# Attention and two MLP layers on one core: a slack before TensorE operations in the planned issue order

## The chip, the cores and the metric

The kernel runs on one core of one Trainium2 chip. The metric is device time in microseconds (us), the median of several runs. A core has five engines that each work through their own queue in order: PE (TensorE, matmuls, with PEld for its weight loads), DVE (VectorE), ACT (ScalarE), POOL (GpSimd) and SP (SyncE, which here issues DMAs). They meet only where one waits for another's result.

## The reference

Attention over 4 batches, 8 heads, 576 positions and 64 dimensions a head. Of each row of scores only those within `tau` of the row's maximum are kept:

```python
scores = scale * np.matmul(q, k.transpose(0, 1, 3, 2))
thresh = np.max(scores, axis=-1, keepdims=True) - tau
scores = np.where(scores >= thresh, scores, -1000000000.0)
attn = np.exp(scores - np.max(scores, axis=-1, keepdims=True))
attn = attn / (np.sum(attn, axis=-1, keepdims=True) + 1e-09)
out = np.matmul(attn, v)
```

The result, 2304 tokens of 512 values, goes through `a = x @ w1; b = x @ w2; x = (a * b @ w3) @ w_out` and then through `h = x @ w_in; x = elu(h) @ w_out2`, with 1024 and 2048 inner columns.

## The kernel before, in words

The attention phase works in 144 tiles of 128 score rows by 576 columns, nine to a pair of heads (16 pairs, `p`), each pair in two parts: n=0 with four tiles, n=1 with five. Four pairs are one batch. The order of the tiles is `SEQ` (lines 329 and 330): the first parts of pairs 0 to 3, then their second parts, then pair by pair.

A tile `i` goes through this chain. S (`emit_S`, matmuls on line 352 for pairs 0 to 3 and on line 364 for the others) writes scores to one of three PSUM buffers `s`. MAX (line 373, VectorE) takes the negated maximum. Two small GpSimd operations make the exponent's bias (line 381, for some tiles) and the threshold (line 377). EXP (lines 386 and 388, ScalarE) and MASK (line 394, VectorE) follow. Then the masked tile is transposed in one of two ways. Most tiles of n=0 go through X (`emit_X`, line 442, five TensorE transposes into the tile's own PSUM buffer) and C (`emit_C`, line 446, a ScalarE copy). Tiles of n=1 of most pairs (`by_dma`) are cast to two halves (line 401 ScalarE, lines 405 and 406 GpSimd) and transposed by DMA (lines 432 and 434, issued by SyncE). In the X way the `s` buffer is free after C, in the DMA way after MASK.

When all tiles of a part are masked, `emit_rr` (lines 454 and 455, VectorE) makes reciprocals of the sums, `turn_r` (line 460, TensorE) turns them, `keep_r` (line 465, ScalarE) copies them out, and SyncE stores them to memory (lines 472 and 474) and loads them back spread over partitions (lines 482 to 488). `emit_PV` (lines 502 and 510, TensorE, in five parts) multiplies with v; `emit_xf` (lines 519 and 521, VectorE) scales by the reciprocals; `emit_xh` (line 527) and `emit_xl` (line 531) split the result for the first MLP layer. The v operand is loaded by `load_v` (line 300), its column sum made by line 305 on ScalarE and brought over partitions by `v_mean` (line 308, TensorE). From pair 4 on, q and k are cast and split (line 284 ScalarE, lines 271, 288 and 292 GpSimd).

The first MLP products ("ab", line 552) of batches 0 to 2 are mixed into the same phase. A product takes 12 matmuls, planned as four operations of three; a batch has 32 of them, 16 for n=0 and 16 for n=1. They need the split results of all four pairs of a batch for that n, and converted weights (lines 205 to 235), and use one of two PSUM buffers `m`, which PV uses as well. They are emptied by line 560 (ScalarE) or line 567 (VectorE). The fourth batch's ab products follow the phase, then the rest (lines 817 to 1095): weights are combined (line 860), the second product (line 1000), and the last two layers (lines 1033 and 1062).

The order of all this is made by `Plan` (lines 57 to 141), in Python, before the kernel is built. Every operation has an engine, an estimated duration `us`, for DMAs a landing time `land`, a priority `key` (lower goes first) and the operations that it depends on. Rings of buffers add dependencies (`take`, `turns`); the two `m` buffers are slots given out when planned (`hold`). `run` then plays the engines forward. Among the operations of an engine that can start at the earliest time (within 0.05 us) it takes the one with the lowest key and issues its instructions (`o.fn()`). When an operation ends, each one that uses it may start no earlier than its end plus `LAT` = 0.15 us across engines or 0.05 us on the same engine (line 137). So the planned times are turned into nothing but an order: on the chip an engine waits for the semaphores of the next instruction in its queue, and what stands behind waits too.

The keys: S has the tile's number `i`, X `i - 2`, C `i - 3`, MASK `i - 2`, PV the number of the part's last tile plus 5, and the ab products of batch 0 have keys that run from 22 to 46 (n=0) and 46 to 78 (n=1), of batch 1 from 78 to 114, of batch 2 from 114 to 150 (lines 776 to 786).

Of the kernel before, what the change touches and what calls it, by code (L numbers as in the profile page):

```python
# [44 lines left out]
FA, FB, FC = (22.0, 24.0), (46.0, 32.0), (6.0, 36.0)  # L45

LAT = 0.15


class Op:  # L50
# [6 lines left out]
class Plan:  # L57
# [30 lines left out]
    def run(self):  # L88
        self.turns()
        for o in self.ops:  # L90
            o.deps = list({id(d): d for d in o.deps if d is not o}.values())
            o.n = len(o.deps)
            for d in o.deps:
                d.outs.append(o)
        place = {id(o): k for k, o in enumerate(self.ops)}
        ready = {}
        free = {}
        for o in self.ops:
            ready.setdefault(o.eng, [])
            free[o.eng] = 0.0  # L100
            if o.n == 0:
                ready[o.eng].append(o)
        done_at = {}
        left = len(self.ops)
        while left:
            best = None
            for e, r in ready.items():
                cand = []
                for o in r:
                    t = max(free[e], o.at)  # L110
                    if o.gets:
                        n, used = self.slots[o.gets]
                        if len(used) >= n:
                            f = done_at.get(id(used[-n]))
                            if f is None:
                                continue
                            t = max(t, f)
                    cand.append((t, o))
                if not cand:
                    continue  # L120
                t0 = min(t for t, _ in cand)
                t, o = min(((t, o) for t, o in cand if t <= t0 + 0.05), key=lambda x: (x[1].key, place[id(x[1])]))
                if best is None or t < best[0]:
                    best = t, o
            t, o = best
            ready[o.eng].remove(o)
            free[o.eng] = t + o.us
            end = t + o.us + o.land
            if o.gets:
                self.slots[o.gets][1].append(o)  # L130
            if o.frees:
                done_at[id(o.frees[1])] = end + LAT
            o.fn()
            o.start = t
            for x in o.outs:
                x.n -= 1
                x.at = max(x.at, end + (LAT if x.eng != o.eng else 0.05) + x.lag)
                if x.n == 0:
                    ready[x.eng].append(x)
            left -= 1  # L140
        self.end = max(free.values())
# [1001 lines left out]
```

## Time and profile before

| | |
|---|---|
| median of 3 runs | 1067.16 us (1064.76 to 1068.95) |
| the profiled execution | 1067.07 us |
| its span in the trace | 1065.0 us |
| instructions | 17060 |
| PE busy | 1014.1 us (95%) |
| PEld busy | 887.0 us (83%) |
| DVE, ACT, POOL busy | 583.6, 514.0, 441.7 us |

The span is the time from the first to the last instruction of the profiled execution. Busy time of PE counts matmuls from start to a modelled end, so that overlapping ones count once. "Idle before" an instruction is time of its engine that ended when the named releaser, an operation on another engine or a DMA, was done. A row of the timeline gives the start in us from the beginning of the span, the duration of a run of equal instructions, the engine, the line, what it writes and reads, the count, and in brackets the idle time just before it with its releaser. `PEclk` is the share of TensorE's full clock that was granted.

### The profile page before, as it was taken

What the parts mean: (1) busy time and instruction counts of PE and PEld (TensorE: products, weight loads), DVE (VectorE), ACT (ScalarE), POOL (GpSimd) and SP (SyncE); (2) the same over time, 40 slices, a digit from 0 to 9 for tenths busy, and PEclk for the clock granted to TensorE, in tenths of its full rate; (3) what the DMA queues carried; (4) which work ended last, traced back from release to release, by engine and by line L of the source; (5) the groups of instructions that cost most, each with busy time, mean ns of one, the idle gap of its engine ahead of it and who ended that gap; (6) DMA issues with size and microseconds to landing.
All of it is one profiled execution on the core that took longest, in us unless ns stands there. A gap on an engine that the chain in (4) does not pass through costs nothing.

```text
span 1065.0 us, 17060 instructions
## 1 busy us (share of the span) xinstructions
PE 1014.1 (95%) x6318; PEld 887.0 (83%) x6318; DVE 583.6 (55%) x1072; ACT 514.0 (48%) x864; POOL 441.7 (41%) x586
## 2 busy tenths in 40 slices
PE   7878999979999999989999999999999999999998
PEld 4445788867888888889879999989999899899997
DVE  4788888764676666646555565843332333323322
ACT  3776777764666665534334555533232232322322
POOL 1648867765657665413321231332222222222221
PEclk8999999998999999999999999999999999999999
DMA  8227688876559444466617673300000000000000
GB/s 264 90 92 197 133 159 137 138 151 158 112 129 160 122 116 87 102 211 211 218 45 242 190 239 110 119 1 30 1 1 30 1 30 1 2 30 1 30 1 30
DMA packets 119726, 109.70 MB, mean 103 GB/s; under 512 B 88176, under 2 KB 106844, under 8 KB 115036
## 3 DMA queue, kind: packets, MB, share of 16 engines
q1 hardware_dynamic: 115532, 78.97, 31.3%
q10 hardware_dynamic: 4112, 29.66, 8.1%
q8 instruction: 49, 0.80, 0.3%
q14 instruction: 33, 0.27, 0.1%
HBM read 73.73 MB, written 14.23 MB: 83 GB/s over the span
## 4 chain that ended last, share of the span: by engine, by line
PE 58%; DMA 1%; issue 1%; POOL 1%; ACT 1%; DVE 1%; SPq 0%; POOLq 0%; ACTq 0%; DVEq 0%
PE h L1033 19%; PE o L1062 19%; PE x L1000 9%; PE ab L552 6%; PE m L860 4%; DMA rb<-rd 1%; POOL hl L405 0%; PE s L364 0%; DMA th<-g_dr 0%; PE s L442 0%; PE pv L502 0%; PE pv L510 0%; DVE sl L200 0%; POOL hl L406 0%; ACT hl L401 0%
## 5 line engine op out<-in xcount | busy, mean ns | idle before, releaser
L552 PE MATMUL ab<-x,W 128*128 128x256 f32 (+1 forms) x1536 | 232.1, 301 | 3.5 <-DVE xf L521 3.5
L552 PEld LDWEIGHTS ab<-x,W 128*128 128x128 f32 x1536 | 211.0, 190 | 10.2 <-issue 3.8
L1062 PE MATMUL o<-WO,sl 128*128 128x512 f32 x864 | 215.7, 394 | 0.6 <-POOL sl L1054 0.6
L1033 PE MATMUL h<-sl,W 128*128 128x384 f32 x1152 | 215.7, 337 | 0.0
L1033 PEld LDWEIGHTS h<-sl,W 128*128 128x128 f32 x1152 | 202.8, 188 | 8.3
L1054 POOL TENSOR_TENSOR sl<-th,sl 128x384 fp32r<-128x384 f32 x87 | 88.4, 1017 | 266.5 <-ACT sl L1049 266.5
L1062 PEld LDWEIGHTS o<-WO,sl 128*128 128x128 f32 x864 | 161.1, 188 | 30.7 <-POOL sl L1054 1.1
L1042 DVE TENSOR_SCALAR th<-h 128x384 f32<-128x384 f32 x96 | 53.3, 555 | 182.8 <-PE h L1033 182.8
L394 DVE SCALAR_TENSOR_TENSOR e<-s,st,e 128x576 f32<-128x576 f32 x144 | 115.3, 814 | 59.2 <-ACT e L388 31.3
L1043 ACT ACTIVATE th<-th 128x384 f32<-128x384 f32 x96 | 50.4, 525 | 194.5 <-DVE th L1042 194.5
L373 DVE TENSOR_REDUCE st<-s 128x1 f32<-128x576 f32 x144 | 106.0, 748 | 23.5 <-PE s L364 7.3
L1000 PE MATMUL x<-sl,M 128*128 128x384 f32 x576 | 101.1, 337 | 0.5 <-ACT sl L199 0.3
L1000 PEld LDWEIGHTS x<-sl,M 128*128 128x128 f32 x576 | 99.6, 188 | 1.9 <-DVE sl L200 0.8
L405 POOL TENSOR_TENSOR hl<-e,hl 128x512 f16<-128x512 f32 x70 | 83.1, 1188 | 24.4 <-ACT hl L401 24.1
L364 PE MATMUL s<-qk 128*128 128x288 f32 x480 | 83.8, 307 | 8.4 <-DVE e L394 4.5
L388 ACT ACTIVATE e<-s,st 128x576 f32<-128x576 f32 x108 | 77.0, 736 | 27.2 <-DVE st L373 17.0
L1049 ACT ACTIVATE sl<-th 128x384 fp32r<-128x384 f32 x96 | 50.4, 525 | 76.7 <-PE o L1062 46.5
L1047 DVE SCALAR_TENSOR_TENSOR th<-th,h 128x384 f32<-128x384 f32 x96 | 53.1, 554 | 58.2 <-ACT th L1043 58.1
L364 PEld LDWEIGHTS s<-qk 128*128 128x128 f32 x480 | 70.1, 192 | 13.3 <-issue 3.8
L442 PE MATMUL s<-ident,e 128*128 128x128 f32 (+1 forms) x370 | 56.1, 284 | 19.5 <-DVE e L394 19.2
L446 ACT ACTIVATE pt<-s 128x640 f32<-128x640 f32 x74 | 51.5, 700 | 45.0 <-PE s L442 36.1
L442 PEld LDWEIGHTS s<-ident,e 128*128 128x128 f32 (+1 forms) x370 | 38.5, 136 | 37.4 <-DVE e L394 32.4
(89 smaller groups left out, 1200.4 us busy)
## 6 DMA issues: line engine op xcount, KB each, us to landing
rqk<-in_qk SPq DMA_DIRECT2D x24, 576.0 KB
raw_wo<-in_wo ACTq DMA_DIRECT2D x12, 1024.0 KB
th<-g_dr SPq DMA_DIRECT2D x48, 192.0 KB
raw_w<-in_w SPq DMA_DIRECT2D x8, 1024.0 KB
raw_w<-in_w3t ACTq DMA_DIRECT2D x8, 1024.0 KB
raw_win<-in_win ACTq DMA_DIRECT2D x8, 1024.0 KB
vr<-in_v SPq DMA_DIRECT2D x16, 320.0 KB
g_dr<-g SPq DMA_DIRECT2D x16, 320.0 KB
```

Of the source, the lines that this page charges most:

```text
L364: T.matmul(s[:, n, :HS], q, k[:, c:c + HS], start=(x == 0), stop=(x == len(ops) - 1))
L373: V.tensor_reduce(st[i][:, 0:1], sc[i][:, :, :HS], axis=AX.XY, op=ALU.max, negate=True)
L388: A.activation(et[i], sc[i][:, :, :HS], AF.Exp, bias=st[i][:, 2:3] if by_dma(i) else st[i][:, 0:1])
L394: V.scalar_tensor_tensor(et[i], sc[i][:, :, :HS], st[i][:, 1:2], et[i], op0=ALU.is_ge, op1=ALU.mult, accum_out=sm[p][:, pos:pos + 1],)
L405: G.tensor_tensor(t[:, S + 64:], e[:, :512], t[:, :512], op=ALU.subtract)
L442: T.transpose(o[:k, c * P:(c + 1) * P], e[:, c * P:c * P + k], ident)
L552: T.matmul(o[:, :w], wf[:, m, wx, kt, :], x[:, xx, :], start=(kt == 0 and k == 0), stop=(kt == NK - 1 and k == 2),)
L1000: T.matmul(o[:, :TB], M[:, f, mx, e * P:(e + 1) * P], gh[j, f][:, gx, :], start=(k == 0), stop=(k == 23),)
L1033: T.matmul(o[:, :TB], WI[f][:, wx, kt, :], xh[j, kt][:, xx, :], start=(k == 0), stop=(k == 3 * NK - 1),)
L1042: V.tensor_scalar(t, o[:, :TB], 0.0, None, op0=ALU.min)
L1054: (V if jobs else G).tensor_tensor(x[:, 1, :], thin[2 + f % 2], f32(x[:, 0, :]), op=ALU.subtract)
L1062: T.matmul(po[j, t], gg[j, f][:, gx, t * P:(t + 1) * P], WO[f // 2][:, f % 2, wx, :], start=(f == 0 and k == 0), stop=(f == NF2 - 1 and k ...
```

## The change

A second constant, `LAG_PE`, is added beside `LAT`. Where an operation on TensorE uses the result of an operation on another engine, its earliest planned start is put 0.8 us later. Slots of `m` (`hold`) and dependencies among other engines keep their times. No instruction is added or removed, and nothing waits for the 0.8 us on the chip: the plan's times change, and with them the order in which the instructions of each engine are issued.

```diff
 LAT = 0.15
+LAG_PE = 0.8
...
             for x in o.outs:
                 x.n -= 1
-                x.at = max(x.at, end + (LAT if x.eng != o.eng else 0.05) + x.lag)
+                wait = LAG_PE if x.eng == "PE" and o.eng != "PE" else 0.0
+                x.at = max(x.at, end + (LAT if x.eng != o.eng else 0.05) + x.lag + wait)
                 if x.n == 0:
                     ready[x.eng].append(x)
```

## Rows read from the trace of the kernel before

**Rows 1.** Stretches of the span: length, busy time per engine, PEclk, DMA share, GB/s.

```profile
0.00:83.00 83.00, 66.47 (x442) 38.83 (x443) 57.97 (x114) 50.40 (x72) 37.67 (x62) 0.96 0.49 156
83.00:213.00 130.00, 121.53 (x933) 98.65 (x933) 105.99 (x219) 94.57 (x156) 101.14 (x165) 0.99 0.76 148
213.00:248.00 35.00, 27.36 (x188) 22.17 (x187) 21.24 (x48) 21.76 (x36) 24.26 (x42) 0.85 0.67 138
248.00:450.00 202.00, 192.40 (x1519) 170.16 (x1519) 135.37 (x302) 124.51 (x218) 120.69 (x204) 1.00 0.58 124
...
475.00:1065.00 590.00, 584.80 (x3087) 536.42 (x3085) 252.23 (x378) 216.38 (x374) 155.46 (x114) 1.00 0.22 72
```

**Rows 2.** The same stretches, the maximum (line 373) alone: DVE busy, one per tile.

```profile
83.00:213.00 130.00, 35.09 (x48) 0.99 0.76 148
213.00:248.00 35.00, 7.82 (x11) 0.85 0.67 138
248.00:450.00 202.00, 45.99 (x63) 1.00 0.58 124
```

**Rows 3.** The third stretch, the ab products (line 552) alone: PE busy, PEld busy.

```profile
213.00:248.00 35.00, 6.18 (x38) 5.62 (x39) 0.85 0.67 138
```

**Rows 4.** Waits of PE, 83 to 213 us: total, times, longest.

```profile
PE s L442 <- DVE e L394: 3.3, 3, 1.9
PE s L364 <- DVE e L394: 2.1, 2, 1.6
PE s L352 <- DVE e L394: 1.4, 1, 1.4
```

**Rows 5.** Waits of PE, 213 to 248 us.

```profile
PE s L364 <- ACT rt L465: 3.4, 1, 3.4
PE s L442 <- DVE e L394: 2.4, 1, 2.4
```

**Rows 6.** Waits of PE, 248 to 450 us.

```profile
PE s L442 <- DVE e L394: 6.2, 9, 1.2
PE s L364 <- DVE e L394: 2.3, 3, 1.1
```

**Rows 7.** Timeline of all engines, 400 to 404 us, the operations around one wait.

```profile
399.36 1.41 DVE L373 TENSOR_REDUCE st<-s 128x1 f32<-128x576 f32 x2
...
400.41 1.43 POOL L288 TENSOR_TENSOR qk<-rqk,qk 64x576 fp32r<-64x576 f32 x1
...
401.94 0.50 POOL L377 TENSOR_SCALAR st<-st,add 128x1 f32<-128x1 f32 x2
402.24 0.82 DVE L394 SCALAR_TENSOR_TENSOR e<-s,st,e 128x576 f32<-128x576 f32 x1 [1.48 <-POOL st L377]
...
403.93 0.70 ACT L446 ACTIVATE pt<-s 128x640 f32<-128x640 f32 x1 [1.96 <-PE s L442]
```

**Rows 8.** Timeline of PE alone, 400 to 428 us, the same wait.

```profile
403.12 1.50 PE L442 MATMUL s<-ident,e 128*128 128x128 f32 x10 [0.91 <-DVE e L394]
404.38 1.12 PE L552 MATMUL ab<-x,W 128*128 128x320 f32 x6
```

**Rows 9.** Timeline of all engines, 15 to 30 us.

```profile
20.35 0.74 ACT L305 ACTIVATE v<-vr 128x640 f16<-128x640 f32 x1 [3.73 <-DMA vr<-in_v]
...
22.54 2.19 PE L352 MATMUL s<-qkp 128*64 128x288 f32 x8 [4.10 <-ACT pt L446]
```

**Rows 10.** Timeline of all engines, 440 to 470 us, the phase's end.

```profile
460.60 0.55 DVE L521 SCALAR_TENSOR_TENSOR xf<-pv,vst,rb 128x320 f32<-128x320 f32 x1 [4.37 <-DMA rb<-rd]
...
461.20 8.99 PE L552 MATMUL ab<-x,W 128*128 128x320 f32 x49 [3.48 <-DVE xf L521]
```

**Rows 11.** One stretch of the last two layers, columns as in rows 1.

```profile
900.00:925.00 25.00, 25.00 (x128) 22.62 (x127) 8.26 (x15) 7.87 (x15) 5.59 (x6) 1.00 0.00 1
```

**Rows 12.** PV (line 502), 0 to 450 us, by shape: count, busy us, mean ns.

```profile
L502 PE MATMUL pv<-pt,vr 128*64 128x256 f32 x256 | 32.9, 393 | 0.6 <-ACT a L560 0.6
...
L502 PEld LDWEIGHTS pv<-pt,vr 128*64 128x64 f32 x288 | 19.1, 139 | 12.8 <-issue 3.2 <-ACT a L560 0.8 <-ACT qk L284 0.4
```

## The prediction

> **What bounds the kernel now.** I read the stages first: busy time and granted clock in six stretches of the span, cut where the kind of work changes [rows 1], then how many score tiles and how many products of the first MLP layer (ab, line 552) fall into each [rows 2, 3], then who makes TensorE wait in each [rows 4 to 6], and last one such wait instruction by instruction [rows 7, 8]. Line numbers are those of the kernel before.
>
> From 475 us on nothing of the changed order is left; TensorE is busy for practically all of that time, and I take it as fixed. The attention phase, up to about 461 us, falls into four parts [rows 1]. Up to 83 us no ab work exists yet; TensorE is idle for 83.0 - 66.5 = 16.5 us. From 83 to 213 us ab products of the first batch fill in; idle 8.5 us. [...] From 248 to 450 us ab work is always at hand; idle 9.6 us at full clock, VectorE only 67% busy (135.4 of 202). The pace is 130 / 48 = 2.7 us a tile in the second part, 35 / 11 = 3.2 in the third and 202 / 63 = 3.2 in the fourth [rows 2].
>
> So the third part shows something the busy shares hide: with less matmul work per tile the tiles do not go faster. There the chain maximum, exponent, mask, transpose sets the pace, not TensorE, and time saved on TensorE before 213 us can be lost again in this gap. Only between 248 and 450 us does a wait on TensorE cost its own length.
>
> What are these waits? Nearly all are a transpose X (line 442) or a score product S (line 364) for VectorE's mask (line 394): 6.2 us in 9 waits and 2.3 us in 3 from 248 to 450, none above 1.2 us [rows 6]; 3.3 + 2.1 + 1.4 = 6.8 us in 6 waits from 83 to 213 [rows 4]. The one at 403 us shows the mechanism: GpSimd is inside a 1.43 us subtraction of line 288, its small threshold operation (line 377) comes behind it, the mask waits for that until 402.24, and X, next in TensorE's order, stands for 0.91 us [rows 7, 8]. Behind it in the same queue lie six ab matmuls that were ready. The planner had put X directly behind the time at which it believed the mask done, and the chip was later than that.
>
> **The change part by part.** It adds nothing to the chip and removes nothing; it alters the order in which instructions enter the queues. In the plan, a TensorE operation becomes ready 0.8 us after the operation on another engine that it uses, on top of the 0.15 us there before. The planner then gives TensorE another ready operation in that time, if it has one. On the chip no instruction waits for this slack: it turns into work in front of X, S, the turn of reciprocals (line 460), the column mean (line 308) and PV. The six ab matmuls behind the wait at 403 take 1.12 us [rows 8], so 0.8 us is about four matmuls, one planner unit of three and a little.
>
> First term, 248 to 450 us: a wait of 0.8 us or less should vanish, a longer one keep its excess. The nine X waits average 0.69 us and the three S waits 0.77; the longest are 1.2 and 1.1 [rows 6]. Excess of up to 0.4 us in perhaps half of them leaves some 1.6 of 8.5 us. Gain 6.9 us. From both sides: all 8.5 if the queue in front is fuller than planned, 0 if the masks come later by as much.
>
> Second term, 83 to 213 us: at most 0.8 us for each of 6 waits, 4.8 us [rows 4]. By the reading of the gap this time comes back as idle time before 248, since the inputs of the next batch come from the tile chain. I take a gain of 1.0 and keep 0 and 4.8 as ends.
>
> Third, 213 to 248 us: the two waits named there are 3.4 us of S for a ScalarE copy and 2.4 us of X for the mask [rows 5]. With no filler at hand the slack moves little: 0, with 2.4 us either way. What covers the moved operations is ab work; in this stretch that cover is gone, and a PV part put in front of X costs its length.
>
> Fourth, up to 83 us: no ab filler either. The large wait (4.10 us at 22.54) is behind ScalarE, which waited 3.73 us for the load of v [rows 9]. Another order on ScalarE could remove that or make a second one; 0, with 4.1 us either way.
>
> Fifth, the end. After the last mask the reciprocals pass TensorE, go out to memory and come back, and VectorE waits 4.37 us for them; TensorE stands idle for 3.48 us before the next ab [rows 10]. That turn now lies up to 0.8 us deeper in the order: loss 0.8, with 0 and 1.6 as ends (the last S may move too). The change of batch inside the long stretch runs through the same chain but has tiles to work on: loss 0.5, between 0 and 1.6.
>
> The other queues move with it. The copies behind X (ScalarE, line 446), the stores of reciprocals and loads behind them (SyncE), xf and its split are planned later, so casts and conversions go ahead of them. A ScalarE copy that falls behind one cast of q and k loses its length at most; where the ring has room this costs nothing, and if that room is gone it is the slower rival below. The DMA transposes follow GpSimd, which gets no slack, and I leave them at zero; SyncE issues in order, so a store of reciprocals that comes later could hold one up, and this is inside the same rival.
>
> Sum: -6.9 - 1.0 + 0 + 0 + 0.8 + 0.5 = -6.6 us. The profiled execution took 1067.07 us (span 1065.0 and 2.1 around it), 0.1 under the median of 1067.16, so no correction is due: **1060.5 us**, 0.6% faster.
>
> [...] By matmul rows, TensorE in 248 to 450 us has 9.6 us to give [rows 1]. Weight loads are busy for 170.2 of these 202 us, 84.2%, while a stretch that never waits shows 22.62 of 25, 90.5% [rows 11]; the difference over 202 us is 12.6 us. I use matmul rows, because the phase has PV products with 64-column weights, which load in 139 ns where the matmul takes 393 [rows 12], so that weight loads idle there without a loss. [...]
>
> **The rivals.** (1) Nothing net, 1067 us. The slack only moves the waits: ab work brought forward is missing afterwards, the gap at 213 us grows by what was saved before it, and the long stretch gets later masks. For it: the gap, in which the tile chain and not TensorE sets the pace. The change could also fail to do what it says: the slack is not added where an ab group waits for its accumulator (the "m" slots), and where one operation alone is ready the order stays. Against it: in 248 to 450 us there is always filler.
>
> (2) Slower, 1076 us: the ring of three score buffers binds. Today an X tile holds its buffer for S (0.6 us by the planner's own cost in line 605) and then from the maximum at 399.36 to the end of the copy at 403.93 + 0.70 = 404.63 [rows 7], 5.9 us in all, 2.0 a tile with three buffers. A slack before X and one before the next S make it 7.5, or 2.5 a tile, against 2.7 a tile from 83 to 213 us and 3.2 later. So there is 0.2 us of room before 213, and none if anything else delays the loop. The price if it binds there: per turn 1.6 / 3 = 0.53 us for the 4 in 9 tiles with an X, 0.27 for the others. 21 x 0.53 + 27 x 0.27 = 18.4 us for 48 tiles, 11.1 if X tiles alone pay. The later gain stays (pace 3.2 against 2.5). Net of -6.9, +0.8 and +0.5 that is 5.5 to 12.8 us slower, 1073 to 1080. It decides from the point at which the loop takes over 8.1 us (three times 2.7).
>
> (3) Larger gain, 1054.8 us: each wait also drains what is behind it, so that the loss is that of the weight loads. For it: weight loads are 6 points short of the dense stretch [rows 1, 11]. Against it: the PV argument.
>
> **How the numbers follow.** The forecast gets 0.47, its own range being 1054 to 1066; rival 1 0.20; rival 2 0.25; rival 3 0.08. A measurement of this kernel tells about 0.5%, 5.3 us, from no change, so faster means below 1061.8: three quarters of the forecast's chance and all of rival 3, 0.43. Same is the rest of the forecast and rival 1, 0.32. Slower is rival 2, 0.25. The range goes from 1054, where the better ends of terms one and two lie (-8.5 - 4.8 + 0.5), to 1076, the middle of rival 2; what lies outside is half of that rival and a little below.
>
> **What the changed profile would show.** If right: the waits of X and S for the mask between 248 and 450 us fall from 8.5 to under 3 us, ab matmuls stand directly in front of X, the stretch from the start of the second batch's ab to the last score tile shrinks by about 7 us, and the time before it stays within 2 us. If rival 1: the waits fall and the gap before the second batch grows by as much. If rival 2: from 83 to 213 us fewer than 48 tiles are done when the first batch's ab ends, and the gap is longer than 40 us. If the large wait near 22 us is gone or another of its size appears before 83 us, the fourth term was wrong, and by that much the time. What would make the prediction wrong outright is a wait for another releaser (ScalarE's copy, the reciprocals) growing where the mask's shrank.

## The result, and the profile after

The changed kernel takes **1073.61 us** (median of 9 runs, 1070.23 to 1078.79) against 1067.37 for the kernel before beside it: a ratio of 1.006 with a 95% interval of 1.0036 to 1.0083. The forecast was 0.6% faster; it became 0.6% slower. The time lies within the stated range, on the side of rival 2. The profiled execution took 1075.75 us, 2.1 above its median, so its differences to the profile before (8.7 us) are somewhat larger than those of the medians (6.2 us). Ratios and their intervals, here and below, leave out two runs that fell into a slow state, one of the kernel before (1079.45 us) and one of experiment 7 (1647.38 us). In the changed kernel all lines of the attention phase have numbers higher by two: MAX is line 375, MASK 396, X 444, C 448, the turn of reciprocals 462, ab 554.

The stretches of [rows 1], in the changed kernel (length, busy time of PE, PEld, DVE, ACT, POOL, granted clock, DMA share, GB/s):

```profile
0.00:83.00 83.00, 66.35 (x408) 39.23 (x408) 56.10 (x106) 47.48 (x68) 29.99 (x61) 0.88 0.48 155
83.00:213.00 130.00, 120.40 (x927) 97.33 (x927) 102.51 (x212) 91.68 (x150) 98.57 (x156) 0.99 0.67 146
213.00:248.00 35.00, 26.58 (x190) 22.41 (x188) 25.10 (x56) 22.92 (x39) 22.23 (x40) 0.90 0.78 128
248.00:450.00 202.00, 191.15 (x1497) 169.89 (x1498) 137.60 (x294) 124.21 (x216) 118.52 (x205) 0.98 0.59 122
```

Up to 83 us TensorE is as busy as before, but did less: 408 matmuls against 442, and the granted clock is 0.88 against 0.96. Cut by work instead of time, from the first ab matmul of the second batch to the first of the fourth, the two kernels look like this, the kernel before first:

```profile
0.00:247.80 247.80, 215.16 (x1557) 159.45 (x1558) 185.00 (x379) 166.53 (x263) 163.06 (x267) 0.96 0.66 149
247.80:461.20 213.40, 200.32 (x1595) 177.35 (x1593) 137.61 (x306) 125.81 (x223) 120.81 (x204) 1.00 0.58 123
```

and the changed kernel:

```profile
0.00:252.90 252.90, 217.07 (x1558) 162.07 (x1558) 187.95 (x379) 166.21 (x262) 155.06 (x264) 0.94 0.63 147
252.90:470.90 218.00, 202.85 (x1595) 179.76 (x1593) 141.27 (x306) 126.62 (x222) 121.16 (x208) 0.98 0.57 120
```

The matmuls of each part are the same in number. The first part is 5.1 us longer and the second 4.6; experiment 1 shows that profiles of one and the same order can differ by 3.4 us in the first part. In the second, 2.5 us are busy time (the same 1595 matmuls at a mean clock of 0.98 instead of 1.00), and 2.1 are idle time: 15.2 against 13.1 us.

Yet the waits that the forecast spoke of did shrink. TensorE's waits from 253 to 452 us, to hold against [rows 6] (total, times, longest; one of PV left out):

```profile
PE s L462 <- DVE st L375: 3.2, 3, 2.0
PE s L444 <- DVE e L396: 2.9, 5, 0.9
PE ab L554 <- ACT a L562: 1.6, 1, 1.6
PE s L462 <- DVE e L396: 1.5, 1, 1.5
```

X waits 2.9 us instead of 6.2, and S (line 366) has left the list. In their place stand 4.7 us of the turn of reciprocals, and 1.6 us of an ab product for its accumulator. One such turn, with VectorE from the timeline of all engines:

```profile
427.60 0.19 DVE L457 RECIPROCAL rr<-rr 128x5 f32<-128x5 f32 x1
...
428.67 0.74 DVE L375 TENSOR_REDUCE st<-s 128x1 f32<-128x576 f32 x1
...
429.47 0.28 PE L462 MATMUL s<-ident,rr 128*5 128x128 f32 x1 [2.02 <-DVE st L375]
```

Its reciprocals were ready at 427.79. It waits for a maximum that ends at 428.67 + 0.74 = 429.41, that of the tile whose PSUM buffer it borrows a corner of. The planner knows of the turn's need of the reciprocals and of S (line 712 in the kernel before), not of this one. In these traces a turn that is issued ahead of that maximum, or long behind it, waits for nothing or little: of the 14 turns between 250 and 450 us none waits over 0.20 us in the kernel before, and ten show no wait in the changed one. The slack brought turns to stand shortly behind. Of the four turns of the long stretch that wait, two (at 293 and 405 us) were issued ahead of the maximum before and are behind it now; the one at 323 us went from behind the tile's exponent to behind its mask, the one at 429 us from behind the mask to between maximum and exponent. The granted clock falls right after it, as it did after the turn at 323 us (windows before and behind the two waits, columns as above):

```profile
320.00:323.00 3.00, 1.70 (x13) 0.69 (x9) 1.95 (x6) 0.97 (x2) 3.00 (x5) 1.00 0.42 96
323.00:328.00 5.00, 4.75 (x26) 4.72 (x27) 2.95 (x8) 2.60 (x5) 3.80 (x5) 0.66 1.04 291
426.00:429.00 3.00, 1.45 (x12) 1.24 (x10) 2.93 (x7) 1.47 (x3) 2.16 (x6) 1.00 0.88 128
429.00:434.00 5.00, 4.53 (x24) 2.91 (x24) 2.01 (x5) 1.15 (x3) 1.50 (x3) 0.66 0.66 134
```

In windows of half a microsecond the granted clock is 1.00 up to 323.5 us, 0.50 from 324.0 to 327.0 and 1.00 again from 327.5; behind the other wait it is 0.50 from 430.0 to 433.0 us and 1.00 from 433.5. An ab matmul of 128x256 takes 0.41 us on the mean from 323 to 328 us and 0.40 from 429 to 434, against 0.29 from 330 to 400 us, at 1.00. From the two windows of 5 us, 5 x 0.34 = 1.7 us of work at full clock are missing each time, an estimate. Before, the whole stretch had 1.00 [rows 1]. The two waits themselves stand in the timeline of TensorE as 2.02 us (the row above) and as this one:

```profile
323.25 0.27 PE L462 MATMUL s<-ident,rr 128*5 128x128 f32 x1 [1.55 <-DVE e L396]
```

Last, the phase's end, where [rows 10] had 3.48 us:

```profile
470.93 9.33 PE L554 MATMUL ab<-x,W 128*128 128x320 f32 x52 [5.18 <-DVE xf L523]
```

### The profile page after: what moved, and what is told of

The parts are those of the page before. It is cut to its first block, busy times and chain, and to the rows that moved or that the text cites. A ratio compares the mean times of both kernels' runs of the same rounds, so it can differ in the third digit from the quotient of the medians.

```text
span 1073.9 us, 17016 instructions
## 1 busy us (share of the span) xinstructions
PE 1018.2 (95%) x6318; PEld 892.0 (83%) x6318; DVE 590.1 (55%) x1072; ACT 514.2 (48%) x864; POOL 433.8 (40%) x586
## 4 chain that ended last, share of the span: by engine, by line
PE 70%; POOL 7%; DVE 7%; DMA 5%; ACT 4%; issue 4%; SPq 1%; DVEq 0%; POOLq 0%; ACTq 0%
PE h L1035 19%; PE o L1064 19%; PE ab L554 11%; PE x L1002 9%; PE m L862 4%; PE s L444 3%; POOL hl L407 3%; DVE e L396 3%; PE s L366 2%; PE s L354 2%; DVE st L375 2%; DMA rqk<-in_qk 2%; POOL qk L290 1%; PE pv L504 1%; ACT e L390 1%
## 5 line engine op out<-in xcount | busy, mean ns | idle before, releaser
L554 PEld LDWEIGHTS ab<-x,W 128*128 128x128 f32 x1536 | 212.6, 191 | 12.6 <-DVE xf L523 5.5
L444 PE MATMUL s<-ident,e 128*128 128x128 f32 (+1 forms) x370 | 60.5, 301 | 16.7 <-DVE e L396 16.6
L444 PEld LDWEIGHTS s<-ident,e 128*128 128x128 f32 (+1 forms) x370 | 43.5, 146 | 32.3 <-DVE e L396 25.7
```

The lines of the kernel that those rows point to most:

```text
L444: T.transpose(o[:k, c * P:(c + 1) * P], e[:, c * P:c * P + k], ident)
L554: T.matmul(o[:, :w], wf[:, m, wx, kt, :], x[:, xx, :], start=(kt == 0 and k == 0), stop=(kt == NK - 1 and k == 2),)
```

## The experiments

All kernels are the changed one with its condition narrowed, some with a dependency added to the plan; the diffs are against it. Differences in us are medians against the median of the kernel before on the same chip. The kernel before and each experiment had 35 and 12 runs; a difference under about 3 us (0.25%) isn't told from none. The ratio on record is not the quotient of the two medians and can differ from it (the late half below: +3.8 us by the medians, and by the ratio of 1.0016 only 1.7 us), so that a size is known no better than this. The theories: **A**, the first half loses because ab work stands in front of S and X from 83 to 213 us; **B**, the turn takes over the waits of the second half; **C**, any other order costs clock at random; **D**, the first 80 us lose because weight conversions get ahead of tiles; **E**, the second half loses at its end.

**1. The two halves.** `end` is the planned end of the operation before; 245 us is where the second batch's ab begins in the plan.

```diff
-wait = LAG_PE if x.eng == "PE" and o.eng != "PE" else 0.0
+wait = LAG_PE if x.eng == "PE" and o.eng != "PE" and end > 245.0 else 0.0    # e3_late
+wait = LAG_PE if x.eng == "PE" and o.eng != "PE" and end <= 245.0 else 0.0   # e4_early
```

> The slack only where the operation before ends after 245 us of planned time, so the order is that of the kernel before until about 248 us. Theory A (the loss is made in the first half, where the tile chain sets the pace and the slack puts work in front of it; the second half gains): 1060 to 1064 us, faster than before by 3 to 7 us. Rival B (in the second half the turn of reciprocals, line 462, waits instead of X and S and eats the gain): 1067 to 1071 us. Rival C (any other order costs some clock dips at random): no rule, within 1067 plus or minus 5.

> The slack only where the operation before ends by 245 us of planned time. Theory A: the loss of the first half stays whole, 1072 to 1077 us, with the second batch's ab starting about 5 us later than before (253 against 248). Rival B: 1067 to 1070 us, since the waits of line 462 after 290 us are gone. Rival C: within 1067 plus or minus 5.

Measured: the late half 1070.65 us, +3.8 (ratio 1.0016, 0.9989 to 1.0044); the early half 1069.53, +2.7 (1.0010, 0.9987 to 1.0034). Their sum by the medians, 6.5, is about the whole change's 6.2; by the ratios it is 2.8, and neither interval excludes no change. Both times lie in B's ranges. So theory A's second sentence falls: the second half does not gain. In the late kernel's profile the waits from 248 to 475 us (those of PV left out) are:

```profile
PE ab L554 <- DVE xf L523: 5.2, 1, 5.2
PE s L462 <- DVE st L375: 2.9, 3, 2.0
PE s L444 <- DVE e L396: 2.5, 5, 0.9
PE s L462 <- DVE e L396: 1.5, 1, 1.5
PE ab L554 <- ACT a L562: 1.4, 1, 1.4
```

It is the pattern of the changed kernel, with a first half ordered as before. X loses 3.7 us of waiting, S 2.3; the turn adds 4.0, the accumulator 1.4, the end 1.7. The long turn waits are at the same places of the order (320 and 425 us), which speaks against chance. The two parts of this profile, cut by work as above:

```profile
0.00:251.20 251.20, 215.05 (x1557) 159.00 (x1558) 185.48 (x379) 166.72 (x263) 162.83 (x267) 0.96 0.66 148
251.20:466.50 215.30, 201.12 (x1595) 178.54 (x1593) 140.02 (x306) 125.22 (x220) 119.73 (x204) 0.99 0.57 121
```

The first part has the order of the kernel before and is yet 3.4 us longer. So most of the 4.5 us by which this profile's span is longer (1069.5 against 1065.0) stands where nothing was changed, and the second part, 215.3 against 213.4 us, accounts for 1.9.

**2. By kind of operation.** The turn and the column mean without slack, and X alone with it. (A function's name is kept with each planned operation as `kind`.)

```diff
-wait = LAG_PE if x.eng == "PE" and o.eng != "PE" else 0.0
+wait = LAG_PE if x.eng == "PE" and o.eng != "PE" and x.fn.kind not in ("turn_r", "v_mean") else 0.0   # e1_no_turn
+wait = LAG_PE if x.eng == "PE" and o.eng != "PE" and x.fn.kind == "emit_X" else 0.0                   # e2_x_only
```

> The slack for every TensorE operation but the turn of reciprocals and the column mean. Theory A: the chain X, S is as slow as in the changed kernel, so 1071 to 1075 us. Rival B: the 10.8 us of waits of line 462 in the changed kernel fall back to about 2, and the time to 1064 to 1068 us. Rival C: within 1070 plus or minus 5.

> The slack for the transposes X alone. Theory A: one of the two slacks in the loop of a score buffer is left, so half the loss, 1069 to 1072 us. Rival B: the turn keeps its place, X waits shrink, 1062 to 1066 us. Rival C: within 1069 plus or minus 5.

Measured: 1075.13 us without the turn's slack, +8.3 (1.0067, 1.0044 to 1.0091), and 1072.29 with X alone, +5.4 (1.0042, 1.0019 to 1.0065). Both lie just over the upper end of theory A's ranges, and B's forecasts are missed by 6 to 7 us. X alone costs nearly as much as all. The profiles put the loss into the first part: the second batch's ab starts at 255.7 us without the turn's slack and at 254.9 with X alone, against 247.8 before and 252.9 in the changed kernel. In the second part of the first of the two kernels the turns after 290 us wait 0.7 us at most, so the slack on the turn does make those waits, and this part takes 5.6 us less than in the changed kernel:

```profile
255.70:468.10 212.40, 200.16 (x1590) 178.54 (x1589) 138.17 (x301) 124.87 (x220) 117.46 (x203) 0.99 0.59 122
```

There B's mechanism holds in this one profile, and the time is lost ahead of it. Just before the second batch's ab one PV product waits 4.2 and 4.5 us for its DMA transposes in these two kernels, against 1.3 before; but it waits 4.6 us also in the second kernel of experiment 3, which gains. With X alone the 25th tile's maximum starts at 85.9 us, hardly later than before (experiment 3), so theory D does not cover this loss. What makes it was not found.

**3. The first half, cut again.** In the first 80 planned us there is practically no ab work.

```diff
-wait = LAG_PE if x.eng == "PE" and o.eng != "PE" else 0.0
+wait = LAG_PE if x.eng == "PE" and o.eng != "PE" and end <= 80.0 else 0.0          # f2_first80
+wait = LAG_PE if x.eng == "PE" and o.eng != "PE" and 80.0 < end <= 245.0 else 0.0  # f3_80_245
```

> The slack only where the operation before ends by 80 us of planned time, where TensorE has no ab work to put in front. Theory A (the first half's loss comes from ab work put in front of S and X between 83 and 213 us): no loss, 1066 to 1068 us. Rival D (the loss comes from the first 80 us: a slower planned tile pace there lets the conversions of the weights, which run by their loads, in ahead of tiles, chunk 6 before mask 21 instead of 25): tile 24 later by about 8 us as in the changed kernel, and 1069 to 1072 us.

> The slack only from 80 to 245 us of planned time, where ab work is at hand. Theory A: 1069 to 1072 us, the second batch's ab 3 to 5 us later than before. Rival D: 1066 to 1068 us, the second batch's ab within 1.5 us of before.

Measured: the first 80 us alone 1069.88, +2.9 (1.0015, 0.9989 to 1.0041); 80 to 245 us alone 1064.21, **-2.8** (0.9980, 0.9958 to 1.0003). Neither interval excludes no change, but the two differ by 5.7 us on one chip, and A asked for the opposite signs. A is out. D has the first time right (1069 to 1072) and had 1066 to 1068 for the second, so that gain was in no theory; of it 1.4 us stand ahead of the second batch's ab in the profile (246.4 us against 247.8) and 1.8 in the second part (211.6 against 213.4). The profiles go with D so far. Weight chunks converted (GpSimd's subtraction, line 237) within the first 100 us, first with the slack in the first 80 us, then with it from 80 on:

```profile
0.00:100.00 100.00, 16.56 (x7) 0.93 0.50 153
```

```profile
0.00:100.00 100.00, 14.19 (x6) 0.93 0.50 148
```

The changed kernel has 7 there and the kernel before 6. The 25th tile's maximum starts at 94.1 us with the slack in the first 80 us and at 95.8 in the changed kernel. In the kernel before it is at 84.6, and in the six experiments whose order begins as before, between 84.6 and 87.1.

**4. The conversions put back.** Each chunk's conversion is held at least until the mask behind which it stood before.

```diff
         ra += [u, w0, w1]
+        for x in (u, w0):
+            pl.after(x, MASK[(2, 4, 8, 11, 16, 18, 25, 27)[f]])
```

`g1_pin_first80` has this and the condition `end <= 80.0`; `g2_pin_all` has it and the whole change.

> The slack up to 80 us of planned time, and the conversion of each weight chunk held behind the mask behind which it stood in the kernel before (masks 2, 4, 8, 11, 16, 18, 25, 27). Rival D: with the conversions back in place tile 24 is within 3 us of before, and the time 1066 to 1069 us. If the order of S and X itself does it: as without the pin, 1069 to 1072 us.

> The whole change, with the conversion of each weight chunk held behind the mask behind which it stood before. Theory D: about 2 to 3 us of the 6.2 go, 1070 to 1072 us, tile 24 no more than 5 us later than before. If the conversions have no part in it: 1073 to 1075 us.

Measured: 1068.09 us (+1.1, 1.0008, 0.9986 to 1.0029) against 1069.88 (+2.9) without the pin, and 1071.95 (+4.9, 1.0055, 1.0031 to 1.0079) against 1073.61 (+6.2). So 1.8 and 1.3 us come back, and the 25th maximum moves from 94.1 to 89.3 and from 95.8 to 92.6 us, half or a third of the way. Both times lie in D's ranges; the tile does not (4.7 and 8.0 us later than before, where D had at most 3 and 5). Neither difference in time leaves the intervals; both go D's way. The 25th maximum is also a poor mark, as VectorE's timeline shows, the kernel before first, then the changed one:

```profile
84.58 0.74 DVE L373 TENSOR_REDUCE st<-s 128x1 f32<-128x576 f32 x1
85.56 0.88 DVE L321 SCALAR_TENSOR_TENSOR v<-vr,vst,v 128x640 f16<-128x640 f32 x1 [0.25 <-ACT v L317]
```

```profile
93.40 2.45 DVE L323 SCALAR_TENSOR_TENSOR v<-vr,vst,v 128x640 f16<-128x640 f32 x1 [0.43 <-ACT v L319]
95.77 0.74 DVE L375 TENSOR_REDUCE st<-s 128x1 f32<-128x576 f32 x1
```

The split of v, which came behind this maximum, now stands ahead of it and takes 2.45 us. At the 29th maximum the delay is 6.5 us in the changed kernel and 7.0 with the slack in the first 80 us; with the pin it is 4.6 and 1.0, where the six kernels that begin in the old order have 0.1 to 2.2. Yet the second batch's ab starts no earlier with the pin: 251.5 against 250.8 us, and 253.1 against 252.9. So the conversions delay the tiles, clearly in the first pair; that they are a part of the loss in time is likely and not shown, and what the rest is stays open. A rival that no run tests is the granted clock up to 83 us: 0.88 in the changed kernel and 0.93 with the slack in the first 80 us, against 0.96 before and 0.92 to 0.96 in the six. Whether it is a cause or goes with the other order is open.

**5. The turn ahead of its tile's maximum.** Late slack, and in the plan the maximum comes after the turn.

```diff
-wait = LAG_PE if x.eng == "PE" and o.eng != "PE" else 0.0
+wait = LAG_PE if x.eng == "PE" and o.eng != "PE" and end > 245.0 else 0.0
...
         ring["s", i] += [tr, kr]
+        if 80 < i < NTILE:
+            pl.after(MAX[i], tr)
```

> The slack from 245 us of planned time on, and in that part the turn of reciprocals (line 462) is planned ahead of the maximum of the tile whose buffer it borrows. Rival B (the turn, issued behind that maximum, waits for it and takes the place of the waits of X and S): its waits go from 4.4 us to under 1, the stretch from the second batch's ab to the fourth's from 215.3 to 210 to 212 us, and the time 1063 to 1067 us. If the long waits are due to the slack itself: 1069 to 1072 us as without it.

Measured: 1071.75 us, +4.7 (1.0034, 1.0014 to 1.0055). The turn's waits for a maximum are gone, as B wanted, and the time does not follow; the stretch from the second batch's ab to the fourth's takes 216.5 us, where B had 210 to 212. TensorE's waits from 248 to 475 us (those of PV left out):

```profile
PE ab L554 <- DVE xf L523: 5.3, 1, 5.3
PE s L444 <- DVE e L396: 3.8, 9, 1.4
PE s L366 <- DVE e L396: 3.6, 1, 3.6
PE ab L554 <- ACT a L562: 0.9, 1, 0.9
PE s L462 <- DVE rr L457: 0.6, 2, 0.3
```

The end's 5.3 us stays, and one S waits 3.6 us for a mask. The timeline of all engines tells why that mask is late:

```profile
355.56 0.74 POOL L273 TENSOR_SCALAR rqk<-rqk,esc 128x576 f32<-128x576 f32 x1 [4.67 <-DMA rqk<-in_qk]
356.38 0.19 POOL L383 TENSOR_SCALAR st<-st 128x1 f32<-128x1 f32 x1
356.61 0.74 ACT L390 ACTIVATE e<-s,st 128x576 f32<-128x576 f32 x1 [3.66 <-POOL st L383]
...
357.45 0.82 DVE L396 SCALAR_TENSOR_TENSOR e<-s,st,e 128x576 f32<-128x576 f32 x1 [2.76 <-ACT e L390]
...
358.33 1.34 PE L366 MATMUL s<-qk 128*128 128x288 f32 x8 [3.58 <-DVE e L396]
```

GpSimd's scaling of q and k waits 4.67 us for its load, the tile's bias (line 383) stands behind it in GpSimd's order, and the exponent, the mask and S wait in turn. With one in-order queue cleared, another stands in the way. That is one profile, 2.7 us under the kernel's median. So the turn's waits are not all that took the gain back; what the kernel would be with them gone and this one too was not tried.

**6. The end planned as before.** The slack stops at 400 planned us; then the same with the gain of experiment 3.

```diff
-wait = LAG_PE if x.eng == "PE" and o.eng != "PE" else 0.0
+wait = LAG_PE if x.eng == "PE" and o.eng != "PE" and 245.0 < end <= 400.0 else 0.0  # h1_245_400
+wait = LAG_PE if x.eng == "PE" and o.eng != "PE" and 80.0 < end <= 400.0 else 0.0   # h2_80_400
```

> The slack from 245 to 400 us of planned time, so the last tiles, the turn that waited 2.0 us at 425 to 429 us and the phase's end are planned as before. Theory E (the second half loses its gain where work is used up: at the end, where ab work brought forward is missing and the wait for the last input grows from 3.5 to 5.2 us, and at the turn before it): the last wait is 3.5 us again, the stretch from the second batch's ab to the fourth's 209 to 212 us against 215.3 with the slack to the end, and the time 1063 to 1067 us. If the loss is spread over the stretch: 1068 to 1071 us.

> The slack from 80 to 400 us of planned time: without the two places that theories D and E name. D and E together: the 2.8 us of the 80 to 245 us run and some gain of the second half, 1059 to 1064 us, faster than both kernels. If the waits of the middle only move: 1064 to 1068 us.

Measured: 245 to 400 us 1067.04, no difference (0.9998, 0.9975 to 1.0021); 80 to 400 us **1063.11**, -3.9 (0.9951, 0.9923 to 0.9980). The wait at the end is 3.4 and 3.3 us, as before. Against the slack to the end (+3.8) the last 60 us of the plan are worth 3.8 us by the medians, on two chips; the second parts of the two profiles differ by 1.8 us (215.3 and 213.5), as much as the wait at the end (5.2 and 3.4). Theory E had the time and the wait right, and had asked for 209 to 212 us in the second part. The second kernel gives the clearest result of all: the same constant costs 6.2 us on the whole plan and gains 3.9 without the first 80 us and what lies behind 400, and both intervals exclude no change. So the loss comes with the slack in one or both of these places, and theory C, that any other order costs, is out. The middle, where the forecast had put nearly its whole gain, gives nothing by itself; TensorE's waits in the first of the two kernels show why (248 to 475 us; the end's wait and those of PV are left out):

```profile
PE s L444 <- DVE e L396: 3.4, 6, 0.9
PE s L462 <- DVE e L396: 1.7, 2, 1.5
PE ab L554 <- ACT a L562: 1.4, 1, 1.4
PE s L462 <- DVE st L375: 0.6, 1, 0.6
```

**7. A smaller slack for S and X alone after 245 us.**

```diff
-wait = LAG_PE if x.eng == "PE" and o.eng != "PE" else 0.0
+wait = (LAG_PE if end <= 245.0 else LAG_PE / 2) if x.eng == "PE" and o.eng != "PE" and (
+    80.0 < end <= 245.0 or end > 245.0 and x.fn.kind in ("emit_X", "emit_S")) else 0.0
```

> The slack of 0.8 us from 80 to 245 us of planned time and then 0.4 us for S and X alone, which leaves every turn of reciprocals but one ahead of its tile's maximum and the end as before. Theory E: X and S waits after 250 us half gone, no long turn wait, 1060 to 1065 us. If the waits only move: 1064 to 1068 us.

Measured: **1061.82 us**, -5.2 (0.9950, 0.9918 to 0.9982), which is faster than both kernels. Its second part, cut by work, and its waits from 248 to 475 us:

```profile
247.50:456.40 208.90, 199.22 (x1590) 177.07 (x1588) 136.48 (x301) 125.07 (x221) 118.12 (x203) 1.00 0.55 125
```

```profile
PE ab L554 <- DVE xf L523: 4.3, 1, 4.3
PE s L444 <- DVE e L396: 4.2, 9, 0.9
PE s L462 <- DVE e L396: 0.4, 1, 0.4
PE ab L554 <- ACT a L562: 0.4, 1, 0.4
```

208.9 us against 213.4, idle 9.7 against 13.1, clock 1.00. Here the waits of X and S fall, 8.5 to 4.2 us, and no turn takes their place: this is the gain that the first term described, at about two thirds of its size (4.5 of 6.9 us) in this profile. One profile does not make that sure: the kernel with the slack in the first 80 us alone has TensorE's order of the kernel before in this part, and took 1.8 us more than that one:

```profile
250.80:466.00 215.20, 202.01 (x1596) 178.75 (x1594) 140.28 (x306) 126.25 (x223) 121.79 (x206) 0.99 0.55 122
```

By the medians this kernel gains 2.4 us over the slack from 80 to 245 us alone, which the intervals do not tell from none. It was run on one setting only; whether 0.4 us or the choice of S and X does it was not separated.

## Why the prediction was wrong

By parts of the plan, from the medians:

| part of the plan | forecast | measured by the slack in that part alone | by the ratio on record |
|---|---|---|---|
| up to 80 us | 0 | +2.9 | +1.6 |
| 80 to 245 us | -1.0 | -2.8 | -2.1 |
| 245 to 400 us | -6.9 (the long stretch to 450) and +0.5 | 0.0 | -0.2 |
| 400 us to the end | +0.8 | +3.8 (late half less 245 to 400) | +1.9 |
| all | -6.6 | +6.2 | +6.4 |

The measured parts add up to 3.9, 2.3 short of the whole, and to 1.2 by the ratios. Some of that is in the first two, which give +0.1 singly and +2.7 together; each part's interval is some 2.5 us wide to either side. So the sizes of the parts are rough, and that they add up is not shown; clear of no change are the whole and the -3.9 us from 80 to 400 us.

**The first term failed** ("a wait of 0.8 us or less should vanish", gain 6.9). The waits did what it said, 8.5 to 2.9 us. The step that failed is the sentence it rests on, "Only between 248 and 450 us does a wait on TensorE cost its own length": that a wait removed from X and S there is time removed from TensorE. With the slack from 245 to 400 us alone these waits fell to 3.4 us and the time did not move (0.0), though 7.5 of the 8.5 us of waits lie before 400 us. The slack moves every operation that depends on another engine, and some of what moves has needs that the planner does not know: the turn falls behind a maximum, an ab product arrives before its accumulator is copied out (no slack there, as rival 1 noted). They gave back 4.3 and 1.6 us in the changed kernel's profile, and behind the two long ones the granted clock fell to 0.66 over 5 us, by the estimate above 1.7 us of work each (not always behind a wait like that at 323 us, as the last section shows). It is what the prediction named as its last sign: a wait for another releaser growing where the mask's shrank. Taking the turn's slack away brought the second part down to 212.4 us in experiment 2, with a loss ahead of it; in experiment 5 another wait appeared. Half the slack on S and X alone brought a gain in experiment 7.

**The fourth term failed** (0 up to 83 us, "no ab filler either"). It looked at what TensorE could put in front. That "casts and conversions go ahead" stands among the prediction's other queues, and is priced at nothing where the ring of buffers has room, without a row for it; that is the step which failed here. A loop with slack takes longer in planned time, while the weight conversions, in the author's reading of the plan, run at the pace of their loads; so per tile more conversions come through, and VectorE, ScalarE and GpSimd get them ahead of tiles that they stood behind before. Up to 85 us GpSimd has begun six chunks in both kernels, and VectorE 25 maxima before against 22 in the changed one. The 25th tile is 11 us later and the 29th 6.5; 5.1 us are left where the second batch's ab begins, 1.7 more than between two profiles of one order (experiment 1). Experiment 4 bears on the conversions: 1.3 to 1.8 us of the time, within its intervals. So the place of this loss is most likely the stretch up to 80 us, and its cause is open.

**The second term** had the right sign (-1.0 against -2.8, with an interval that reaches just past 0). In its profile 1.4 us are saved by the start of the second batch's ab, about what the term had; the rest came later, from a part it did not speak of. **The fifth** had the mechanism and was too small: the wait at the end grew by 1.7 us where 0.8 was taken, the ends having been 0 and 1.6. The second part of the late half has a granted clock of 0.99 where before it was 1.00, and the turn wait of 2.0 us lies in the same last stretch. No run isolates the term's other 0.5 us, the change of batch.

**Rival 2** had the sign, 0.25, but not the place: it put the loss between 83 and 213 us, where the slack gains. **Rival 1** was right for 245 to 400 us: nothing net, as the waits move. X and S lose 5.1 us of waiting, but the idle time of the second part falls only by 0.8 (12.3 against 13.1 us), and its busy time grows by 1.0 (201.3 against 200.3), at a mean clock of 0.99. **Rival 3** priced the long stretch at 12.6 us, the difference of the weight-load shares, in place of the 6.9 of the first term, and came to 1054.8 us so. No run shows that these 12.6 us can be had; the best kernel took 4.5 out of the second part. The share of weight loads over that part agrees in direction: it is 83.1% before (177.35 of 213.40), 82.5% after (179.76 of 218.00) and 84.8% in experiment 7 (177.07 of 208.90), in the order of the times. It is no independent test, since the loads take nearly the same time in all three.

## What to carry to other kernels

A wait removed from one instruction of an in-order engine is only worth its length if what comes next can run; here X and S lost 5.6 us of waiting, and the turn and the accumulator gained 5.9. List what else the same change moves, and for each moved operation every dependence that it waits for on the chip, also those that the planner was never told (here the turn's for a maximum, 2.02 us). A slack in a planner is not local: it stretches planned time, and what runs by another measure (here the weight conversions) slides against the rest. Try such a change by stretches of the plan: here one constant cost 6.2 us on the whole plan and gained 3.9 on its middle, and the sum told nothing of either. And compare two profiles of one order before reading anything from a stretch: here they differed by 3.4 us.

## What the runs showed of the hardware that was not expected

A single wait of TensorE of 1.55 or 2.02 us, with the engine busy on both sides of it, was followed by a fall of the granted clock (0.66 over the next 5 us, 0.50 for about 3 of them); so was the 3.58 us of experiment 5 (0.66 from 358 to 363 us). Single waits of up to 1.2 us in the long stretch before were not (1.00 over 202 us [rows 1]). Length alone did not decide: in the kernel with the slack from 80 to 400 us an S waits 1.86 us at 306 us, and the clock stays at 1.00 behind it:

```profile
306.00:311.00 5.00, 4.59 (x36) 4.54 (x37) 4.70 (x10) 4.84 (x9) 3.00 (x7) 1.00 1.11 140
```

Nor did the order of the instructions. The late half (experiment 1) and the slack from 245 to 400 us (experiment 6) have one order up to 400 planned us, and in both the turn at 320 us waits 1.47 us. The 5 us behind it, in the late half first:

```profile
320.37 0.27 PE L462 MATMUL s<-ident,rr 128*5 128x128 f32 x1 [1.47 <-DVE e L396]
320.00:325.00 5.00, 4.63 (x39) 4.64 (x40) 3.82 (x9) 2.74 (x6) 4.04 (x6) 1.00 1.08 298
```

```profile
320.22 0.27 PE L462 MATMUL s<-ident,rr 128*5 128x128 f32 x1 [1.47 <-DVE e L396]
320.00:325.00 5.00, 4.78 (x27) 4.78 (x28) 2.78 (x8) 2.61 (x5) 3.75 (x5) 0.66 1.03 292
```

It is the same wait as the one of 1.55 us at 323 us in the changed kernel. In these runs a wait could thus cost nearly twice its length (2.02 us, and behind it 1.7 us by the estimate from the clock) or its length alone, and for one and the same order it could be either.
